# Attention and states @ w1 in small array tiles, x turned on VectorE, every engine in text order, the last states' round in a branch

## The chip, the core and the metric

One core of one Trainium2 chip. The metric is the device time of one execution in microseconds (us); the kernel before took 625.12 (median of 3 runs, 624.7 to 626.98).

## What is computed

```python
# attention block: B=8, H=8, S=512, Ns=32, D=64
scores = 0.125 * x @ state^T            # per (b, h): 512 x 32
xread  = softmax(scores, over states) @ state        # 512 rows per batch
sread  = softmax(scores^T, over tokens) @ x          # 32 rows per batch
rows   = concat([xread, sread], axis=2), heads side by side   # 8 x 544 rows of 512
# routing: E=8 experts, F=1024
logits = rows @ w_gate                  # 512 x 8
e      = argmax(logits);  gw = softmax(logits)[e]
out    = gw * (relu(rows @ w1[e]) @ w2[e])           # w1[e]: 512 x 1024, w2[e]: 1024 x 512
```

All in float32. With the seeded inputs all 512 x rows of a batch go to one expert, and the 256 state rows go to the eight experts as 32, 120, 0, 29, 1, 40, 0, 34. In groups of up to 32 rows of one expert that is 11 groups.

## The kernel before

**Attention** (`front`, `back`, L340 to L366). For each batch, x lies in SBUF with 128 tokens a row (`load_x`, L172, packets of one head's 64 numbers) and is turned on TensorE, 16 transpositions of 128x128 into one PSUM buffer, each four of them copied out on ScalarE (`transpose_x`, L194). The states of a batch are turned on TensorE into `stT`, in which two heads share a 128x64 block with zeros in the other halves (`prep_state`); `scores` multiplies each such block with the turned x into `pc`. `read_weights` makes the softmax over states (32x32 block transpositions and full-width operations on VectorE, exp on ScalarE, one product on GpSimd) and `write_weights` that over tokens. `back` turns the second softmax on TensorE (`transpose_write`), multiplies it with x (`write_rows`, `pw`) and stores the rows to DRAM (`st_dram`, L258), and forms the gate logits of the x rows (`logits_x`, `pl`). `route` and `choose` give each batch its expert `eb`; SyncE reads it into a register (L323) and loads that expert's w1 and w2 (L332, L336).

**Feed-forward of a batch** (`batch`). xread @ w1 is not formed directly: `states_w1` multiplies the states with w1 into `G` (`pG`), `up` multiplies `G` with the softmax (`ph`), and `down` multiplies the result with w2 (`py`). Each 512-column product shows as two MATMULs of 512 columns in the trace.

**State rows.** After all batches' attention, `logits_s` reads the state rows back (`srow`), a rank among the rows of each expert sends them by indirect DMA to slots in `ss_dram`, and four rounds of 128 slots (four groups of 32) run through their own experts' weights: `round_x` turns the rows, `round_up` (`pgh`) and `round_down` (`pgy`) multiply with tiles `s` of four experts (1 MB each, four DMAs on SyncE's queue), four w1 buffers (`S1B`) and three w2 buffers (`S2B`).

**Order.** Only TensorE's instructions keep their text order (`mm`, `tp`, L124, L127); the other engines' are placed by the planner. The attention of batches 0 and 1 runs ahead of the first feed-forward. That of batches 2 to 7 is a generator whose pieces are put between the matmuls of `up` (after each `f`) and `down` (after every second `f`) of batches 0 and 1; what is left of it, `logits_s`, the ranks and the scatter stand after batch 1. The four rounds are a second generator, put between the matmuls of batches 2 to 7. A branch at the end handles x rows whose expert is not their batch's; none are there.

Of the kernel before, what the change touches and what calls it, by code (L numbers as in the profile page):

```python
# [20 lines left out]
def kernel(  # L21
# [15 lines left out]

    nc = tc.nc

# [17 lines left out]
    S1B, S2B = 4, 3  # L57
# [10 lines left out]

    ident = const.tile([128, 128], FP32)
    masks.make_identity(nc, ident[:])  # L70
    iota_p = const.tile([128, 1], FP32)
    nc.gpsimd.iota(iota_p[:], pattern=[[0, 1]], base=0, channel_multiplier=1,
                   allow_small_or_imprecise_dtypes=True)
    colf = const.tile([128, 128], FP32)
    nc.gpsimd.iota(colf[:], pattern=[[1, 128]], base=0, channel_multiplier=0,
# [3 lines left out]
    nc.vector.tensor_scalar(U128[:], colf[:], iota_p[:, 0:1], None, ALU.is_gt)  # L79
    ones_b = const.tile([128, 128], BF16)  # L80
    nc.gpsimd.memset(ones_b[:], 1.0)
    rev8 = const.tile([128, E], FP32)
    nc.gpsimd.iota(rev8[:], pattern=[[-1, E]], base=E, channel_multiplier=0,
                   allow_small_or_imprecise_dtypes=True)
    io8 = const.tile([128, E], FP32)
    nc.gpsimd.iota(io8[:], pattern=[[1, E]], base=0, channel_multiplier=0,
                   allow_small_or_imprecise_dtypes=True)
    jio = const.tile([128, NG], FP32)
    nc.gpsimd.iota(jio[:], pattern=[[1, NG]], base=0, channel_multiplier=0,
# [3 lines left out]
    nc.gpsimd.iota(tok_x[:], pattern=[[SO, B], [1, NC]], base=0, channel_multiplier=NC)  # L93
# [3 lines left out]
    nc.vector.tensor_scalar(quad[:], iota_p[:], 32.0, None, ALU.is_ge)  # L97
    for q in (64.0, 96.0):
        nc.vector.tensor_scalar(tmp_p[:], iota_p[:], q, None, ALU.is_ge)
        nc.vector.tensor_tensor(quad[:], quad[:], tmp_p[:], ALU.add)  # L100
    tok_s = const.tile([128, NST], I32)
    nc.vector.tensor_scalar(tmp_p[:], quad[:], float(SO - NS), iota_p[:, 0:1], ALU.mult, ALU.add)
    for g in range(NST):
        nc.vector.tensor_scalar(tok_s[:, g:g + 1], tmp_p[:], float(4 * g * SO + S), None, ALU.add)

    wg = const.tile([128, NDC, E], FP32)
    nc.scalar.dma_start(out=wg[:], in_=moe_w_gate.rearrange("(c p) e -> p c e", p=128))


    aT = const.tile([128, B, 2, S], FP32)  # L110
    stT = const.tile([128, B, NPR, 2 * NS], FP32)
    NX = B * NC
    lg = const.tile([128, NX + NST, E], FP32)
# [8 lines left out]
    def mm(*args, **kw):  # L122

        tc.keep_in_program_order(nc.tensor.matmul(*args, **kw))  # L124

    def tp(*args):
        tc.keep_in_program_order(nc.tensor.transpose(*args))  # L127

    turn = [0]

    def evict(dst, src):

        turn[0] += 1
        if turn[0] % 2:
            nc.scalar.copy(dst, src)
        else:
            nc.vector.tensor_copy(out=dst, in_=src)  # L137


    ffn = tc.alloc_tile_pool(name="ffn", bufs=1)  # L140
    ps_h = tc.alloc_tile_pool(name="ps_h", bufs=2, space=PSUM)
    ps_y = tc.alloc_tile_pool(name="ps_y", bufs=2, space=PSUM)


    att = tc.alloc_tile_pool(name="att", bufs=2)
    ps_c = tc.alloc_tile_pool(name="ps_c", bufs=1, space=PSUM)
    ps_m = tc.alloc_tile_pool(name="ps_m", bufs=1, space=PSUM)
    ps_s = tc.alloc_tile_pool(name="ps_s", bufs=1, space=PSUM)


    st2 = att.tile([128, B * 2, 2, D], FP32, bufs=1)
    st_rows = state.rearrange("b (g i) n d -> (i n) (b g) d", g=2)
    for u in (slice(0, 2), slice(2, 2 * B)):
        for k in range(2):
            nc.scalar.dma_start(out=st2[:, u, k, :], in_=st_rows[:, u])
    nc.vector.memset(stT[:], 0.0)
    gst = att.tile([128, B, 2, E], FP32, bufs=1)


    blank = att.tile([128, XW], I32, bufs=1)  # L160
    nc.gpsimd.memset(blank[:], 0)
    nc.gpsimd.memset(blank[:, DM + 1:DM + 2], FAR)
    for r in range(NR):
        nc.scalar.dma_start(out=ss_dram[ts(r, 128)], in_=blank[:])

    x_nat = {}

    def load_x(b):

        x_nat[b] = att.tile([128, NC, H, D], FP32, tag="x", bufs=3, name="x_nat")  # L170
        for c in range(NC):
            nc.sync.dma_start(out=x_nat[b][:, c],  # L172
                              in_=x[b].rearrange("h (p c) d -> p c h d", c=NC)[:, c])

    def prep_state(b):
        pt = ps_m.tile([128, 2, 2, 2, NS], FP32, tag="m", name="pt")
        for g in range(2):
            tp(pt[:, g], st2[:, 2 * b + g], ident[:])
        for i in range(2):

            evict(stT[ts(i, 64), b].rearrange("p (g j) n -> p g j n", g=2)[:, :, :, ts(i, NS)],
                  pt[ts(i, 64), :, :, i, :])

        pg = ps_s.tile([128, 2, E], FP32, tag="s", name="pg")
        for j in range(NPR):
            mm(pg[ds(64 * (j % 2), 64), j // 2, :], lhsT=stT[:, b, j, :], rhs=wg[:, j, :],
                             start=True, stop=True, skip_group_check=True)
        evict(gst[:, b], pg[:])

    def transpose_x(b, xT, j):  # L190
        pt = ps_m.tile([128, NC, 128], FP32, tag="m", name="pt")
        for c in range(NC):
            tp(pt[:, c, :], x_nat[b][:, c, ts(j, 2), :], ident[:])
        nc.scalar.copy(xT[:, j], pt[:])  # L194

    def scores(b, xT):

        pc = ps_c.tile([128, 2, S], FP32, tag="c", name="pc")
        for j in range(NPR):
            mm(pc[ts(j % 2, 64), j // 2, :], lhsT=stT[:, b, j, :], rhs=xT[:, j],  # L200
                             start=True, stop=True, skip_group_check=True)
        return pc

    def read_weights(b, pc):

        NB = 2 * S // 32
        sx = att.tile([128, NB, NS], FP32, tag="sx", name="sx")
        nc.vector.transpose(sx[:].rearrange("p b n -> p (b n)"), pc[:].rearrange("p g s -> p (g s)"))
        mx = att.tile([128, NB, 1], FP32, tag="mx", name="mx")
        nc.vector.tensor_reduce(mx[:, :, 0], sx[:], AX.X, ALU.max)  # L210
        nc.vector.tensor_tensor(sx[:], sx[:], mx[:].to_broadcast([128, NB, NS]), ALU.subtract)
        nc.scalar.activation(sx[:], sx[:], AF.Exp, bias=0.0, scale=SCALE)
        sm = att.tile([128, NB, 1], FP32, tag="sm", name="sm")
        nc.vector.tensor_reduce(sm[:, :, 0], sx[:], AX.X, ALU.add)
        nc.vector.tensor_scalar(sm[:], sm[:], 1e-9, None, ALU.add)
        nc.vector.reciprocal(sm[:], sm[:])  # L216
        nc.gpsimd.tensor_tensor(sx[:], sx[:], sm[:].to_broadcast([128, NB, NS]), ALU.mult)  # L217
        nc.vector.transpose(aT[:, b].rearrange("p g s -> p (g s)"), sx[:].rearrange("p b n -> p (b n)"))  # L218

    def write_weights(pc):  # L220

        nm = att.tile([128, 2], FP32, tag="nm", name="nm")
        nc.vector.tensor_reduce(nm[:], pc[:], AX.X, ALU.max)
        nc.vector.tensor_scalar(nm[:], nm[:], -SCALE, None, ALU.mult)
        a2 = att.tile([128, 2, S], FP32, tag="a2", name="a2")
        s2 = att.tile([128, 2], FP32, tag="s2", name="s2")
        for g in range(2):
            nc.scalar.activation(a2[:, g], pc[:, g], AF.Exp, bias=nm[:, g:g + 1], scale=SCALE,
                                 accum_out=s2[:, g:g + 1])
        nc.vector.tensor_scalar(s2[:], s2[:], 1e-9, None, ALU.add)  # L230
        nc.vector.reciprocal(s2[:], s2[:])
        return a2, s2

    def transpose_write(a2):

        a2T = att.tile([128, 2, NC, 128], FP32, tag="a2T", name="a2T")
        for g in range(2):
            pt = ps_m.tile([128, NC, 128], FP32, tag="m", name="pt")
            for c in range(NC):
                tp(pt[:, c, :], a2[:, g, ts(c, 128)], ident[:])  # L240
            nc.scalar.copy(a2T[:, g], pt[:])  # L241
        return a2T

    def write_rows(b, a2T, s2):


        pw = ps_s.tile([128, 2, 2, D], FP32, tag="s", name="pw")
        for g in range(2):
            for c in range(NC):
                for i in range(2):  # L250
                    mm(pw[ts(i, 64), g], lhsT=a2T[:, g, c, ts(i, 64)],
                                     rhs=x_nat[b][:, c, ts(2 * g + i, 2), :],
                                     start=(c == 0), stop=(c == NC - 1), skip_group_check=True)
        xs = att.tile([128, 2, 2, D], FP32, tag="xs", name="xs")
        for g in range(2):
            nc.vector.tensor_scalar(xs[:, g], pw[:, g], s2[:, g:g + 1], None, ALU.mult)
        for i in range(4):
            nc.scalar.dma_start(out=st_dram[ts(b, NS)].rearrange("n (g i d) -> n g i d", g=2, i=4)[:, :, i, :],  # L258
                                in_=xs[ts(i, NS), :, i % 2, :])
# [80 lines left out]
    def front(b):  # L340

        xT = att.tile([128, NPR, NC, 128], FP32, tag="xT", bufs=1, name="xT")
        for j in range(NPR):
            transpose_x(b, xT, j)
            yield
# [420 lines left out]
```

## Time and profile before

| | us |
|---|---|
| profiled execution, device time | 626.47 |
| its span, first to last instruction | 624.6 |
| TensorE MATMUL busy (2225) | 541.8 (87%) |
| VectorE / ScalarE / GpSimd busy | 132.1 / 109.3 / 23.4 |
| `py` / `ph` MATMULs busy | 234.8 (512) / 119.4 (256) |
| `pgh` / `pgy` MATMULs busy | 35.4 (256) / 31.7 (256) |
| `pG` MATMULs busy | 32.4 (128) |
| mean granted TensorE clock | 0.947 |
| HBM read and written | 123 MB, 197 GB/s over the span |

Busy time of a group counts overlapping MATMULs once; the mean duration of one is longer than its share, since the array is pipelined. PEclk is the granted clock: 1.00 is 2.4 GHz, 0.50 is 1.2 GHz, and what lies between is a mean over a stretch. DMA share is the mean busy share of 16 DMA engines.

### The profile page before, as it was taken

Reading aid. Unit: us, or ns where it says so; the run is one execution under the profiler, and the core shown is the slowest. Engines: PE = TensorE matmul, PEld = TensorE weight load, DVE = VectorE, ACT = ScalarE, POOL = GpSimd, SP = SyncE. Lnnn points to the kernel's source line nnn. Section 1 sums busy time; section 2 is a strip of 40 time slices with the busy share of each in tenths; the row PEclk is TensorE's granted clock in tenths of the full one; section 3 lists DMA queues with packets and bytes.
Section 4 is the critical chain, followed back from the end, with each engine's and each line's share of the span. In section 5 each row is a group of like instructions: output and inputs, shape, how many; then the busy total and the mean of one; then the engine's idle time right before and its main releaser. Section 6 shows DMA issues by size and latency. Waiting matters only on the chain.

```text
span 624.6 us, 6270 instructions
## 1 busy us (share of the span) xinstructions
PE 541.8 (87%) x2225; PEld 241.4 (39%) x2225; DVE 132.1 (21%) x287; ACT 109.3 (17%) x202; POOL 23.4 (4%) x29
## 2 busy tenths in 40 slices
PE   1674798988979894858599999999999999999997
PEld 0354344554535552413133343333433333333343
DVE  1245234524634240220001100110011002000100
ACT  1322133324323211110001101110011101101100
POOL 1011001011010010010000000000000000000000
PEclk9967799999999997797989999999999999999999
DMA  9416920464404004049898987999899879534601
GB/s 239 98 41 166 388 89 1 105 206 143 115 6 151 23 20 171 0 168 309 296 356 284 371 318 233 299 356 335 285 323 372 284 271 324 188 115 173 198 25 44
DMA packets 96497, 123.15 MB, mean 197 GB/s; under 512 B 45775, under 2 KB 45775, under 8 KB 96464
## 3 DMA queue, kind: packets, MB, share of 16 engines
q1 hardware_dynamic: 83552, 110.65, 53.6%
q10 hardware_dynamic: 12432, 11.04, 5.3%
q0 software_dynamic: 480, 1.05, 0.5%
q8 instruction: 18, 0.29, 0.2%
q14 instruction: 15, 0.12, 0.1%
HBM read 111.69 MB, written 11.54 MB: 197 GB/s over the span
## 4 chain that ended last, share of the span: by engine, by line
PE 77%; issue 8%; DMA 7%; ACT 4%; DVE 2%; SPq 1%; ACTq 1%; POOL 0%; POOLq 0%; DVEq 0%
PE py L124 34%; PE ph L124 16%; PE pgh L124 6%; PE pgy L124 5%; PE pt L127 5%; PE pG L124 4%; PE pw L124 3%; PE pc L124 2%; DMA w1t<-in_moe_w_dram 2%; PE pl L124 2%; DMA s<-in_moe_w_dram 1%; DMA ss_dram<-blank 1%; DMA ss_dram<-srow,slot_i 1%; ACT xT L194 1%; ACT a2T L241 1%
## 5 line engine op out<-in xcount | busy, mean ns | idle before, releaser
L124 PE MATMUL py<-w2t,hT 128*128 128x512 f32 x512 | 234.8, 604 | 0.0
L124 PEld LDWEIGHTS py<-w2t,hT 128*128 128x128 f32 x512 | 94.0, 192 | 119.7 <-issue 119.7
L124 PE MATMUL ph<-aT,G 128*128 128x512 f32 x256 | 119.4, 610 | 0.0
L124 PEld LDWEIGHTS ph<-aT,G 128*128 128x128 f32 x256 | 47.3, 194 | 59.7 <-issue 58.7
L449 ACT ACTIVATE y<-py,gw 128x512 f32<-128x512 f32 x32 | 22.0, 687 | 223.6 <-PE py L124 211.7
L405 DVE TENSOR_SCALAR hT<-ph 128x512 f32<-128x512 f32 x31 | 21.4, 691 | 153.4 <-PE ph L124 153.4
L124 PE MATMUL pgh<-s,sxT 128*32 128x512 f32 x256 | 35.4, 620 | 6.7 <-DMA s<-in_moe_w_dram 6.7
L127 PE MATMUL pt<-ident,x_nat 128*128 128x128 f32 x128 | 23.2, 306 | 18.3 <-ACT xT L194 9.5
L403 ACT ACTIVATE hT<-ph 128x512 f32<-128x512 f32 x33 | 19.7, 597 | 93.1 <-PE ph L124 93.1
L124 PE MATMUL pG<-w1t,stT 128*64 128x512 f32 x128 | 32.4, 633 | 3.5 <-DMA w1t<-in_moe_w_dram 2.3
L124 PE MATMUL pgy<-s,shT 128*32 128x512 f32 x256 | 31.7, 599 | 0.0
L127 PEld LDWEIGHTS pt<-ident,x_nat 128*128 128x128 f32 x128 | 17.0, 154 | 34.1 <-issue 16.6
L194 ACT COPY xT<-pt 128x512 f32<-128x512 f32 x32 | 18.7, 584 | 32.4 <-PE pt L127 32.4
L217 POOL TENSOR_TENSOR sx<-sx,sm 128x1024 f32<-128x1024 f32 x8 | 15.3, 1912 | 209.1 <-DVE sm L216 186.5
L124 PE MATMUL pl<-gst,aT 128*128 128x8 f32 x128 | 17.1, 270 | 6.0 <-DVE aT L218 6.0
L124 PEld LDWEIGHTS pl<-gst,aT 128*128 128x128 f32 x128 | 16.6, 209 | 11.5 <-issue 11.5
L124 PE MATMUL pw<-x_nat,a2T 128*64 128x128 f32 x256 | 18.9, 311 | 1.7 <-DVE gst L137 1.4
L124 PEld LDWEIGHTS pgh<-s,sxT 128*32 128x32 f32 x256 | 7.9, 111 | 31.9 <-issue 17.6
L127 PE MATMUL pt<-ident,a 128*128 128x128 f32 x64 | 11.5, 306 | 9.6 <-ACT a2T L241 5.4
L124 PEld LDWEIGHTS pw<-x_nat,a2T 128*64 128x64 f32 x256 | 16.9, 159 | 3.3 <-DVE gst L137 1.8
L124 PEld LDWEIGHTS pG<-w1t,stT 128*64 128x64 f32 x128 | 7.8, 141 | 24.7 <-DVE G L137 7.6
L124 PE MATMUL pc<-xT,stT 128*64 128x512 f32 x64 | 17.3, 665 | 0.0
(114 smaller groups left out, 237.8 us busy)
## 6 DMA issues: line engine op xcount, KB each, us to landing
s<-in_moe_w_dram SPq DMA_DIRECT2D x256, 256.0 KB, 5.2
w1t<-in_moe_w_dram SPq DMA_DIRECT2D x8, 2048.0 KB, 9.5
w2t<-in_moe_w_dram SPq DMA_DIRECT2D x8, 2048.0 KB, 10.9
x_nat<-in_x_dram SPq DMA_DIRECT2D x32, 256.0 KB, 4.0
out_dram<-y ACTq DMA_DIRECT2D x32, 256.0 KB, 4.5
ss_dram<-blank ACTq DMA_DIRECT2D x4, 257.0 KB, 6.3
xg<-ss_dram SPq DMA_DIRECT2D x4, 257.0 KB, 3.3
st<-in_state_dram ACTq DMA_DIRECT2D x2, 448.0 KB, 8.7
```

Of the source, the lines that this page charges most:

```text
L124: tc.keep_in_program_order(nc.tensor.matmul(*args, **kw))
L127: tc.keep_in_program_order(nc.tensor.transpose(*args))
L194: nc.scalar.copy(xT[:, j], pt[:])
L217: nc.gpsimd.tensor_tensor(sx[:], sx[:], sm[:].to_broadcast([128, NB, NS]), ALU.mult)
L241: nc.scalar.copy(a2T[:, g], pt[:])
L403: nc.scalar.activation(dst, src, AF.Relu)
L405: nc.vector.tensor_scalar(dst, src, 0.0, None, ALU.max)
L449: nc.scalar.activation(y[:], py[:], AF.Copy, scale=gw[:, NC * b + c, :])
```

## The change

- All engines' instructions go through `InOrder`, which keeps them in text order.
- x is loaded in packets of 1 KB, two DMAs a batch, and turned in 32x32 blocks by VectorE; no TensorE transposition and no ScalarE copy is left for it. The states are loaded four times over (with halves swapped in every second copy) and turned by VectorE.
- Scores: 64 products of 32x32 tiles with 128 columns for each batch in place of 4 of 128x64 with 512. `pw`: 32 products with 32 columns of weights and 64 columns of x in place of 16 of 64 and 128. `pl`: the gate's table is the weight and the softmax the moving side, 8 products of 128 columns, and VectorE turns the result. `pg` and `pG`: 64x32 tiles, `pG` 16 products of 512 columns a batch in place of 8.
- PSUM: four banks for `pG`, `ph`, `py` together, four for the attention (`pa`).
- relu runs on ScalarE alone. In attention behind the first three fronts a subtraction moves from VectorE to GpSimd.
- Batches 0 and 1 choose their expert ahead of their state rows. Attention 2 to 7, `logits_s`, ranks, scatter and the rounds are one generator (`others`); its pieces stand after every fourth matmul of `down` and every second `f` of `up` of all eight batches: 12 a batch.
- Three rounds run always; the fourth stands in a branch that is taken when there are more than 12 groups. `S1B` goes from 4 to 3.

```diff
+        def __getattr__(self, name):
+            def call(*args, **kw):
+                ins = getattr(self.engine, name)(*args, **kw)
+                tc.keep_in_program_order(ins)
+                return ins
+            return call
...
+    NRS = 3
+    S1B, S2B = 3, 3
...
+    def load_x(b):
+        x_nat[b] = att.tile([128, H, NC, D], FP32, tag="x", bufs=2, name="x_nat")
+        for h in (slice(0, 4), slice(4, 8)):
+            sp.dma_start(out=x_nat[b][:, h].rearrange("p h c d -> p h (c d)"),
+                         in_=x[b, h].rearrange("h (p c) d -> p h (c d)", c=NC))
...
+    load_x(0)
+    load_states(0, 1)
+    load_x(1)
...
+    def front(b, early):
+
+        xt = att.tile([128, H, NC, 2, 32], FP32, tag="xt", name="xt")
...
+            if h.start == 4:
+                dve.transpose(stT[:, b].rearrange("p h u n -> p (h u n)"),
+                              st4[:, ts(b, H)].rearrange("p h d -> p (h d)"))
+            dve.transpose(xt[:, h].rearrange("p h c u t -> p (h c u t)"), x_nat[b][:, h].rearrange(flat))
+            yield
+
+        for q in range(4):
+            for g in range(2):
+                pe.matmul(pa[ts(q, 32), 2 + g, 1, 0:E], lhsT=stT[ts(g, 64), b, 2 * q + g, 0, :],
+                          rhs=wg[ts(g, 64), q, :], start=True, stop=True, skip_group_check=True)
         for g in range(2):
...
+            for u in range(2):
+                for q in range(4):
+                    for i in range(4):
+                        pe.matmul(pa[ts(q, 32), i, 0, ts(g, 128)],
+                                  lhsT=stT[ts(i, 32), b, 2 * q + g, u ^ (i % 2), :],
+                                  rhs=xt[ts(i, 32), 2 * q + g, :, u, :],
+                                  start=(u == 0), stop=(u == 1), skip_group_check=True)
...
+                for q in range(4):
+                    pe.matmul(pw[ts(q, 32), g], lhsT=a2T[:, g, c, ts(q, 32)], rhs=x_nat[b][:, 2 * q + g, c, :],
+                              start=(c == 0), stop=(c == NC - 1), skip_group_check=True)
...
+        for q in range(4):
+            sp.dma_start(out=st_dram[ts(b, NS), ts(q, 128)], in_=xs[ts(q, 32)].rearrange("p g d -> p (g d)"))
+        if b + 2 < B:
+            load_x(b + 2)
...
+        for g in range(2):
+            for i in range(4):
+                pe.matmul(pl[ts(i, 32)], lhsT=gst[:, b, g, :], rhs=aT[:, b, i, g, :],
+                          start=(g == 0), stop=(g == 1), skip_group_check=True)
+        dve.transpose(lg[:, ts(b, NC)].rearrange("p c e -> p (c e)"), pl)
...
+        for k in range(2):
+            pg = [ps_p.tile([128, 512], FP32, tag="p", name="pG") for _ in range(2)]
+            for q in range(4):
+                for g in range(2):
+                    pe.matmul(pg[g][ts(q, 32), :], lhsT=st[ts(g, 64), 2 * q + g, 0, :],
+                              rhs=w1t[ts(g, 64), q, ts(k, 512)], start=True, stop=True, skip_group_check=True)
...
+            if insert and f % 2:
                 insert()
...
+                if insert and f == 3:
                     insert()
...
+            for k in range(NDC):
+                round_up(r, k)
+                fetch(2, 0)
+                yield
+                if k % 2:
+                    yield
+            round_h(r)
+            yield
+            for f in range(0, NFC, 2):
+                for i in range(2):
+                    round_down(r, f + i)
+                    fetch(0, 1)
+                yield
+                if f % 4:
+                    yield
...
+    for _ in front(0, True):
+        pass
+    for _ in run(front(1, True), back(0, True)):
+        pass
     e0 = expert_of(eb, 0)
     load_w1(0, e0)
     load_w2(0, e0)
+    for _ in run(front(2, True), back(1, True)):
+        pass
     load_w2(1, expert_of(eb, 1))
...
+        for b in range(2, B):
+            yield from run(*([front(b + 1, False)] if b + 1 < B else []), back(b, False))
+        yield from logits_s()
+        yield from sort_states()
+        change_pools()
+        yield from rounds(0, NRS)
...
+        with tc.If(number(more_i, NG) > 0):
+            for _ in rounds(NRS, NR):
+                pass
```

In text order, `front` of the first two batches and `back` go on as: full-width VectorE steps of the first softmax, the second softmax's exps on ScalarE, then for `back(0)` the turned softmax, logits, `route`, `choose`, and after the scores of the next batch the state rows, their four stores and the next `load_x`, all three on SyncE's queue ahead of the first w1.

## Rows read from the trace of the kernel before

**Rows 1.** Busy time by stretch: engines' busy us (instructions), granted clock, DMA share, GB/s.
```profile
0.00:67.50 67.50, 33.06 (x188) 22.54 (x188) 25.32 (x72) 14.32 (x29) 5.92 (x17) 0.80 0.60 154
67.50:236.00 168.50, 154.04 (x789) 80.91 (x790) 68.21 (x134) 50.32 (x101) 11.47 (x6) 0.99 0.32 104
236.00:320.00 84.00, 56.91 (x175) 24.50 (x174) 9.94 (x40) 7.10 (x12) 2.13 (x2) 0.80 0.62 209
350.00:500.00 150.00, 148.54 (x557) 55.21 (x559) 15.33 (x22) 18.59 (x30) 1.96 (x2) 1.00 0.91 316
```
**Rows 2.** The same for single tiles: py twice, ph twice, pG, pgh.
```profile
67.50:236.00 168.50, 59.93 (x128) 22.39 (x128) 4.81 (x7) 0.99 0.32 104
236.00:320.00 84.00, 20.89 (x42) 8.55 (x42) 2.06 (x3) 0.80 0.62 209
67.50:236.00 168.50, 30.44 (x65) 11.19 (x66) 5.52 (x8) 4.78 (x8) 0.99 0.32 104
236.00:320.00 84.00, 16.51 (x32) 6.76 (x31) 2.08 (x3) 2.98 (x5) 0.80 0.62 209
67.50:236.00 168.50, 13.21 (x48) 3.20 (x48) 4.15 (x6) 3.40 (x6) 0.99 0.32 104
236.00:320.00 84.00, 10.43 (x48) 2.40 (x48) 0.00 (x0) 0.00 (x0) 0.80 0.62 209
```
**Rows 3.** The chain of waits inside the first feed-forward batches: start us, us, what.
```profile
74.81 0.44 PE pt L127 x4
75.25 1.72 PE ph L124 x4
...
84.40 0.41 PE pg L124 x8
84.81 1.91 PE ph L124 x4
86.72 1.87 PE pc L124 x8
...
107.29 1.97 PE pw L124 x32
...
113.04 1.88 PE pl L124 x16
```
**Rows 4.** Tile pgh in slices of 10 ns, where one group of four tiles begins.
```profile
378.27:378.28 0.01, 0.00 (x1) 0.00 (x1) 0.00 (x0) 0.00 (x0) 1.00 0.00 0
...
378.29:378.30 0.01, 0.01 (x4) 0.01 (x4) 0.00 (x0) 0.00 (x0) 1.00 0.00 0
```
**Rows 5.** Timeline of the start: start us, us, engine (q: its DMA queue), line, operation.
```profile
1.28 3.83 ACTq L155 DMA_DIRECT2D st<-in_state_dram  x4
...
5.62 8.28 ACTq L164 DMA_DIRECT2D ss_dram<-blank  x4
...
29.65 1.24 DVE L208 STREAM_TRANSPOSE sx<-pc 128x1024 f32<-128x1024 f32 x1
...
54.63 0.14 DVE L320 CAST eb<-eb_f 128x1 int32<-128x1 f32 x1
...
57.70 0.39 SPq L332 DMA_DIRECT2D w1t<-in_moe_w_dram  x1
...
67.54 5.36 PE L124 MATMUL pG<-w1t,stT 128*64 128x512 f32 x16 [2.34 <-DMA w1t<-in_moe_w_dram]
```
**Rows 6.** The chain of waits again, from the scatter into the rounds.
```profile
272.79 7.53 DMA ss_dram<-srow,slot_i
...
304.87 6.71 DMA s<-in_moe_w_dram
...
323.42 1.85 PE pgh L124 x16
```
**Rows 7.** DMA issues of the rounds' weight tiles: count, KB each, us to landing.
```profile
s<-in_moe_w_dram SPq DMA_DIRECT2D x256, 256.0 KB, 5.2
```

More of the change, by code (lines that the diff above doesn't have):

```diff
@@ L134, in evict @@
         if turn[0] % 2:
-            nc.scalar.copy(dst, src)
+            act.copy(dst, src)
         else:
[L137 to L162, printed above, removed]
@@ L190, in transpose_x @@
[L190 to L202, printed above, removed]
@@ L286, in route @@
+        yield
+        for t in range(NST):
+            for c in range(NDC):
+                pe.matmul(pl[:, t, :], lhsT=sT[:, t, c, :], rhs=wg[:, c, :],
+                          start=(c == 0), stop=(c == NDC - 1), skip_group_check=True)
+        dve.tensor_copy(out=lgs[:], in_=pl)
+        route(lgs[:], NX, NST)
+        yield
+    def route(lg, u0, U):
         r = slice(u0, u0 + U)
         mx = att.tile([128, U, 1], FP32, tag="r_mx", bufs=1, name="r_mx")
-        nc.vector.tensor_reduce(mx[:, :, 0], lg[:, r], AX.X, ALU.max)
+        dve.tensor_reduce(mx[:, :, 0], lg, AX.X, ALU.max)
@@ L386, in run @@
             yield
-    def attention(b0, b1):
-        yield from front(b0)
-        for b in range(b0, b1):
-            yield from run(*([front(b + 1)] if b + 1 < b1 else []), back(b))
-            finish(b)
     def no_dep(d):
@@ new lines, with change_pools, round_in @@
+    late = {}
+    def change_pools():
+        ps_a.release()
+        att.release()
+        late["sst"] = tc.alloc_tile_pool(name="sst", bufs=1)
+        late["ps_g"] = tc.alloc_tile_pool(name="ps_g", bufs=1, space=PSUM)
+        late["ps_t"] = tc.alloc_tile_pool(name="ps_t", bufs=1, space=PSUM)
+    rd = [dict() for _ in range(NR)]
+    def round_in(r):
+        xg = late["sst"].tile([128, XW], FP32, tag="xg", bufs=2, name="xg")
+        sp.dma_start(out=xg[:].bitcast(I32), in_=ss_dram[ts(r, 128)])
+        rd[r].update(xg=xg, e=[expert_of(eg, 4 * r + q) for q in range(4)])
@@ new lines, in round_w1, with round_w2 @@
+    def round_w1(r, k, half):
+        t = late["sst"].tile([128, 4, 512], FP32, tag="s1", bufs=S1B, name="s1")
+        for q in range(4):
+            sp.dma_start(out=t[:, q], in_=moe_w1[ds(rd[r]["e"][q], 1), ts(k, 128), ts(half, 512)]
+                              .rearrange("o p f -> p (o f)"))
+        rd[r][1, k, half] = t
+    def round_w2(r, f):
+        t = late["sst"].tile([128, 4, DM], FP32, tag="s2", bufs=S2B, name="s2")
+        for q in range(4):
+            sp.dma_start(out=t[:, q], in_=moe_w2[ds(rd[r]["e"][q], 1), ts(f, 128), :]
+                              .rearrange("o p f -> p (o f)"))
+        rd[r][2, f] = t
@@ new lines, in round_x, with round_up @@
+    def round_x(r):
+        pt = late["ps_t"].tile([128, NDC, 128], FP32, tag="t", name="ptx")
+        for c in range(NDC):
+            pe.transpose(pt[:, c, :], rd[r]["xg"][:, ts(c, 128)], ident[:])
+        xT = late["sst"].tile([128, NDC, 128], FP32, tag="sxT", bufs=2, name="sxT")
+        evict(xT[:], pt[:])
+        rd[r]["xT"] = xT
+        rd[r]["ph"] = [late["ps_g"].tile([128, 512], FP32, tag="g", bufs=2, name="pgh") for _ in range(2)]
+    def round_up(r, k):
+        for half in range(2):
+            for q in range(4):
+                pe.matmul(rd[r]["ph"][half][ts(q, 32), :], lhsT=rd[r]["xT"][:, k, ts(q, 32)],
+                                 rhs=rd[r][1, k, half][:, q, :], start=(k == 0), stop=(k == NDC - 1),
+                                 skip_group_check=True)
@@ L482, in batch @@
             hT = up(G, aT[:, b + 1], piece)
+    work = others()
     G = states_w1(w1s[0], stT[:, 0])
@@ L486 @@
     hT = up(G, aT[:, 0], piece)
-    batch(0)
-    batch(1)
+    for b in range(B):
+        batch(b)
     for _ in work:
@@ L493 @@
     left = const.tile([128, 1], FP32)
[L494 removed]
+    dve.tensor_reduce(left[:], cmx[:, :, 0], AX.X, ALU.add)
     left_i = const.tile([128, 1], I32)
[L496 to L505 removed]
@@ L735 @@
+    for pool in (late["ps_t"], late["ps_g"], late["sst"], ps_p, ffn):
         pool.release()
```

712 lines of the change are left out of this document (321 added, 391 removed).

## The prediction

> **What bounds the kernel now.** I read the page first (TensorE busy 87%, the others near 20%), then the span by stretch, because a mean over stages with different limits says nothing [rows 1]. Four stretches: to 67.5 us TensorE is busy half the time at a mean clock of 0.80, ahead of the first product with w1; to 236 us it works at full clock on batches 0 and 1 with the attention of 2 to 7 between; to 320 us it is busy 56.9 of 84 us at 0.80; from there it is full (148.5 of 150 us) at 316 GB/s, and so to the end. So TensorE's own work is the bound outside two stretches, and there it waits for chains. Next the single tiles in these stretches [rows 2], the chain of waits inside the feed-forward [rows 3], the start's timeline [rows 5] and the chain around the scatter [rows 6].
>
> The unit: four MATMULs of 512 columns take 1.72 us [rows 3], 0.43 each.
>
> **The change part by part.** The sum is made against the profiled execution: 626.5 us, span 624.6.
>
> *Start.* Before, ScalarE issues DMAs until 5.62 + 8.28 = 13.9 us, and eb, w1's issue and the first product stand at 54.6, 57.7 and 67.5 [rows 5]. After, ScalarE has 17 issues instead of 9; four cost 3.83 [rows 5], so I put its first work at 18 us (14 to 22). Then in text order, each full-width step at the 1.24 of the block transposition [rows 5]: the exp, the sum and the product of the softmax with small steps, 5 us; x(1)'s first half and the turned softmax, 2.5; logits, route and choose with some 15 small steps of 0.2, 4.5: eb stands near 30. But SyncE reads it only behind batch 0's stores, and these wait for the scores of batch 1 and four more full-width steps (32 to 40), so w1 is issued near 46 instead of 57.7. Its landing, 10 us [rows 5], isn't last any more: ahead of the first product TensorE has the scores of batch 2 in its order, whose x is issued behind the stores at about 43 and lands some 5 us later; x, the turned softmax, batch 1's logits and choice, and the second half of x follow on VectorE one after another, to 56, and the scores with `pw` end near 59. First product at 59 (55 to 67): **-8.5 us**.
>
> *Attention among the feed-forward.* From 67.5 to 236 TensorE does 128 + 65 products of 0.43 = 83.0 and 13.2 of `pG` [rows 2]. The rest of the 168.5, 72.3 us or 12 a batch, is attention and what it makes TensorE wait. A batch has 16 transpositions of x (four cost 0.44), the states' turn with its wait for two copies, `pc` 1.87, `pw` 1.97, `pl` 1.88 and the transpositions of the second softmax [rows 3]. After: no transposition of x or states. Scores are 64 products, so 128 MATMULs of 128 columns, 0.43 / 4 = 0.11 each alone. No row shows tiles with fewer than 128 rows. The nearest is `pgh`, four column tiles at once: 16 MATMULs in 1.85 [rows 6], begun within 30 ns of each other [rows 4]. With four at a time the scores take 128 x 0.11 / 4 = 3.5 us, with 16 at a time 0.9; I take 1.2, since starts at most 10 ns apart leave 128 of them 1.3 at most. `pw`: 64 MATMULs of 64 columns, four at a time, 0.9 to 1.0. `pl`: 16 of 128 columns, four at a time, 0.45 (its 1.88 is loads of 128 columns of weights for 8 columns of work). `pg` 0.3 (0.41 now), the eight transpositions 0.9, the count 0.1. Each return from small tiles to full ones costs 1.91 - 1.72 = 0.2 [rows 3], five or six a batch: 1.2. That makes 5.2 a batch; six batches less one front are 30: **-42** (-46 to -27).
>
> The Trainium skill says the opposite of a free mix: a change of tiling mode, not of the tile alone, drains TensorE (TensorEngine Tiling (Array Packing), Key Properties). Here a drain is no more than the 0.2 of the first `ph` behind `pg`; by the rule with that row the new 64x32 and 32x32 blocks add six such drains a batch, the 1.2 above, and nothing else.
>
> VectorE takes 3 us a batch more for x and states (1.24 for 1,024 columns), on a stretch where it is busy 68 of 168 us; ScalarE loses four copies and gets the other half of the relus. Six pieces a batch of 3.4 us of matmuls cover both. If that cover goes, `scores` waits, the third rival.
>
> *States @ w1.* `pG` is 16 MATMULs a batch; of three in 13.2 us the first took 5.4 at a low clock [rows 2, 5], so 3.9 when warm. After: 32 of 512 columns in 64x32 tiles, eight at a time, 32 x 0.43 / 8 = 1.7 and a switch, 1.9. If row halves take turns it is 3.4. Eight batches save 16, less 1 for a first one that is still cold: **-15** (-16 to -2).
>
> *Between batch 1 and the rounds.* From 236 to 320 TensorE does 42 + 32 products of 0.43 = 31.8, `pG` 3.9, 48 MATMULs of `pgh` 5.6 [rows 2, 6], in all 41.6 with the first turn of rows. So 42.4 us are lost: the state rows' way through DRAM, the scatter (7.53) and first weight tiles (6.71) [rows 6], and half clock behind the gaps. After, that chain lies between matmuls of batches 2 and 3. 96 pieces stand in the text (4 in the first `up`, 8 in each `down`, 4 in each further `up`); the generator needs 87, of which 35 attention, 6 logits and ranks, 3 spare pieces ahead of the rounds. So nothing is left over at the end. 3.5 us of logits and turns remain. What is late next are weight tiles. The first four of w1 need a buffer that the first product frees, behind three tiles of w2: as now, 7. Then with three buffers the second half of the next step's w1 is fetched only when the step's first half is done. It has one piece (3.44) and two halves of 0.93, 5.3 us, where 1.3 us of issue and 5.2 of landing are needed [rows 7]; steps with two pieces have 8.7. 12 of 24 steps are short by about 1.3: 15 us (0 to 45). Remaining 25.5: **-17** (-35 to +10). The DMA rate itself suffices: 50 MB of three rounds, 11 of batches' weights and 6 of rows in about 215 us are 312 GB/s, where 316 ran without a stop [rows 1].
>
> *Fourth round.* 11 groups fit into three rounds. A round is eight blocks of 16 MATMULs at 1.85 [rows 6], 12 transpositions at 0.11, two waits for a copy and eight returns of 0.2, 19 us, all between dense matmuls: **-19** (-16 to -20). Relu of a round on ScalarE alone, one after the other at TensorE's cost: **+2**.
>
> *Text order.* Nothing is queued past what waits, so a late step holds its whole engine. Where pieces are 3.4 us apart most steps are done a piece early; I take **+5** (0 to 30) for the rest.
>
> Sum: -8.5 - 42 - 15 - 17 - 19 + 2 + 5 = -94.5. 626.5 - 94.5 = 532.0; the median of the runs is 1.4 below the profiled one: **530 us**.
>
> **The rivals.**
> 1. *Weight tiles bound the rounds.* All 24 steps wait, the short ones for 3 us, the long ones for 1, instead of 15 in all 48: +33, 563. For it: the buffers went from four to three and pieces came closer. Against it: in 350 to 500 TensorE kept 99% at 316 GB/s [rows 1].
> 2. *Row groups take turns*, only column tiles run at once: scores 3.5 instead of 1.2, `pG` 3.4 instead of 1.9, eight batches: +30, 560. For it: no row shows two row groups. Against: the tiles' results go to different PSUM banks.
> 3. *Text order holds the engines.* The start gains nothing (+8.5) and each of six attention batches stops four pieces by 0.7 us, about half a full-width step of VectorE (+17): +25, 555.
> 4. *One tile at a time*, at the scores and `pG`: 128 x 0.11 and 32 x 0.43 are 13.8 us each, `pw` 3.5, `pl` 1.7, in all 33 a batch instead of 4.6. Eight batches: +227, 757, slower than before. It decides from below two tiles at a time on: 33 / 1.9 is 17.3 a batch, 102 us over the forecast, and all is gone. Against: four column tiles do run at once [rows 4], so row tiles would have to break that.
> 5. *A fixed cost per instruction.* If each MATMUL cost 62 ns, 128 scores would be 7.9 us: +54, 584. [rows 4] show four begun in 30 ns, and eight of `pg` with their weights took 0.41 [rows 3], which leaves it one chance in a hundred. The Trainium skill gives these 62 ns as what the sequencer spends on a MATMUL where hardware decode is off (TensorE: Matmul & The Clock Gate, "Wait — 56ns, not 53.3ns?"); by that rule the forecast would be 584, and the trace speaks against its condition.
> 6. *The branch is taken* (the change wouldn't do what it says): a round's 16.8 MB alone at 316 GB/s is 53 us with nothing beside it: 583. The routing counts above exclude it unless float rounding moves a row; one in a hundred.
>
> **How the numbers follow.** Chances: forecast 0.64, weights 0.12, row groups 0.10, text order 0.10, one tile 0.02, fixed cost 0.01, branch 0.01. The range goes down to 500, where start, attention and weights all come out at their good ends (-4, -4, -17, and text order free, -5), and up to 566, beyond the first three rivals. Faster by over 0.5% (about what a measurement here can tell from no change) is all but the one-tile case and a remainder: 0.97; same 0.01; slower 0.02.
>
> **What would show it.** Start: the first `pG` near 59. Attention: the scores' 128 MATMULs of a batch in about 1.2 us; 3.5 says rival 2, 14 rival 4. `pG` 1.9 a batch. Middle: no stretch with TensorE below 90% between the first product and the end but for waits on `s`, in sum near 22 us, and no half clock there. Rounds: 192 MATMULs of `pgh`, not 256. Wrong would be: the first product at 67 or later; waits on `s` above 40 us; TensorE waiting for VectorE's turned x in the feed-forward; any `pgh` behind the last `py`.

## The result, and the profile after

The changed kernel takes 608.24 us (median of 4 runs, 605.07 to 611.25), beside 626.05 for the kernel before on the same chip: 0.971 of it (0.966 to 0.977), 18 us faster. The forecast was 530, with a range of 500 to 566. The sign was right; 78 of the 96 us forecast did not come. The profiled execution took 607.1 us, its span is 605.3.

The span by stretch, with the columns of [rows 1]; the stretches are the start, the attention of batches 2 to 7, the sort, the first round's products with w1, the rest of the rounds, the end.

```profile
0.00:79.60 79.60, 20.66 (x616) 15.32 (x616) 40.87 (x91) 10.66 (x21) 2.09 (x15) 0.98 0.63 160
79.60:306.00 226.40, 193.67 (x1748) 91.66 (x1752) 78.30 (x176) 54.38 (x104) 19.11 (x10) 0.92 0.31 107
306.00:325.00 19.00, 19.00 (x77) 8.09 (x62) 5.50 (x30) 2.76 (x5) 2.13 (x2) 1.00 0.62 214
325.00:383.00 58.00, 46.97 (x173) 15.86 (x171) 2.08 (x3) 9.48 (x16) 0.00 (x0) 0.91 0.88 303
383.00:562.70 179.70, 171.72 (x666) 61.63 (x665) 6.34 (x9) 25.15 (x41) 1.96 (x2) 0.99 0.78 264
562.70:605.30 42.60, 37.98 (x90) 16.58 (x88) 1.15 (x4) 6.33 (x10) 0.98 (x1) 1.00 0.08 29
```

TensorE stands still in three places: the start is 12 us longer than before, the attention stretch has gaps and a clock of 0.92, the first round waits. The same for `py` and `ph` alone, as in [rows 2]:

```profile
79.60:306.00 226.40, 89.26 (x192) 36.65 (x192) 8.24 (x12) 0.92 0.31 107
79.60:306.00 226.40, 64.54 (x128) 25.87 (x128) 19.11 (x32) 0.92 0.31 107
```

320 products of 0.43 are 137.6 us, and four and a half `pG` of 1.9 some 8.5; 80 of the 226.4 us are attention and its waits, where the terms had 30 and 3.5. One of five equal places, TensorE's timeline (in brackets the idle time ahead and who ended it):

```profile
96.83 0.27 PE L48 MATMUL pa<-wg,stT 64*32 64x8 f32 x16
97.03 1.90 PE L48 MATMUL pa<-xt,stT 32*32 32x128 f32 x128
103.15 0.75 PE L48 MATMUL pa<-aT,gst 128*32 128x128 f32 x16 [4.21 <-DVE nm L48]
103.83 5.24 PE L48 MATMUL ph<-aT,G 128*128 128x512 f32 x8
111.09 0.24 PE L48 MATMUL pa<-oh,ones_b 128*128 128x8 bf16 x4 [2.02 <-ACT a L48]
```

The logits (`pa<-aT,gst`) need nothing of `nm`, the maxima over the scores just computed. But these belong to the next batch, lie in the first halves of the same four banks of `pa`, and the logits are written into a second half. VectorE shows what TensorE sat through:

```profile
99.17 1.44 DVE L48 STREAM_TRANSPOSE sx<-pa 128x256 f32<-128x256 f32 x4 [5.30 <-ACT gst L48]
100.65 1.22 DVE L48 TENSOR_REDUCE mx<-sx 128x32 f32<-128x1024 f32 x1
101.78 1.22 DVE L48 TENSOR_REDUCE nm<-pa 128x2 f32<-128x1024 f32 x1
```

The next eight `ph` then took 5.24 us instead of the 3.7 that they take at full clock behind small tiles, at a granted clock of 0.70. What TensorE waited for, over the whole span (us, times, longest), and in the last line the copies `a2T` in the attention stretch alone:

```profile
PE pa L48 <- DVE nm L48: 21.1, 5, 4.2
PE pa L48 <- ACT sx L48: 10.9, 2, 5.4
PE pa L48 <- ACT a2T L48: 7.0, 10, 0.7
PE pa L48 <- ACT a L48: 6.7, 3, 2.6
...
PE pa L48 <- ACT a2T L48: 4.2, 6, 0.7
```

The waits for `nm` and `a` all stand in the attention stretch, the two for `sx` at the start.

At the start [rows 5], ScalarE's queue, its first copy `gst`, then the table's `eb`, w1's issue and the first product:

```profile
0.76 5.39 ACTq L48 DMA_DIRECT2D st<-in_state_dram  x6
7.11 0.40 ACTq L48 DMA_DIRECT2D wg<-in_moe_w_gate_dram  x1
7.55 13.52 ACTq L48 DMA_DIRECT2D st<-in_state_dram  x6
21.16 2.62 ACTq L48 DMA_DIRECT2D ss_dram<-blank  x4
...
25.16 0.17 ACT L48 COPY gst<-pa 128x16 f32<-128x16 f32 x1
...
40.58 0.15 DVE L48 CAST eb<-eb_f 128x1 int32<-128x1 f32 x1
41.45 0.39 SPq L48 DMA_DIRECT2D w1t<-in_moe_w_dram  x1
...
76.43 1.22 DVE L48 TENSOR_REDUCE nm<-pa 128x2 f32<-128x1024 f32 x1
76.55 1.06 ACT L48 ACTIVATE sx<-sx 128x1024 f32<-128x1024 f32 x1 [4.02 <-DVE sx L48]
77.75 1.93 PE L48 MATMUL pa<-x_nat,a2T 128*32 128x64 f32 x64 [5.44 <-ACT sx L48]
79.62 3.62 PE L48 MATMUL pG<-w1t,stT 64*32 64x512 f32 x32
```

The view puts the wait of `pw` down to ScalarE's exp `sx`, which neither reads `pa` nor makes anything that `pw` needs. `nm` reads `pa` and ended 0.04 us later (77.65 and 77.61).

In the rounds, the idle time ahead of instructions on tile `s`, and a piece of the chain of waits [rows 6]:

```profile
  DMA s<-in_moe_w_dram: 41.8, 35
```
```profile
331.60 6.35 DMA out_dram<-y
...
340.95 6.48 DMA s<-in_moe_w_dram
347.48 1.91 PE pgh L48 x2
349.39 3.64 PE py L48 x8
```

### The profile page after: what moved, and what is told of

Same layout as the page of the kernel before. It is cut to its first block, busy times and chain, and to the rows that moved or that the text cites. A ratio compares the mean times of both kernels' runs of the same rounds, so it can differ in the third digit from the quotient of the medians.

```text
span 605.3 us, 8328 instructions
## 1 busy us (share of the span) xinstructions
PE 490.0 (81%) x3353; PEld 209.1 (35%) x3353; DVE 134.2 (22%) x312; ACT 108.8 (18%) x197; POOL 26.3 (4%) x30
## 4 chain that ended last, share of the span: by engine, by line
PE 69%; DMA 12%; DVE 8%; ACT 4%; ACTq 3%; SPq 2%; issue 2%; POOL 0%; POOLq 0%; DVEq 0%
PE py L48 33%; PE ph L48 17%; PE pa L48 8%; DMA s<-in_moe_w_dram 7%; PE pgy L48 4%; PE pG L48 3%; PE pgh L48 3%; ACTq L48 3%; DVE sx L48 3%; DMA out_dram<-y 2%; SPq L48 2%; DVE mx L48 2%; DVE nm L48 1%; DMA st<-in_state_dram 1%; ACT a2T L48 1%
## 5 line engine op out<-in xcount | busy, mean ns | idle before, releaser
L48 ACT ACTIVATE hT<-ph 128x512 f32<-128x512 f32 x64 | 38.2, 597 | 115.2 <-PE ph L48 115.2
L48 PE MATMUL pa<-aT,gst 128*32 128x128 f32 x128 | 7.4, 369 | 49.0 <-DVE aT L48 28.0
L48 DVE COPY G<-pG 128x512 f32<-128x512 f32 x16 | 10.8, 687 | 65.1 <-PE pG L48 65.0
L48 DVE STREAM_TRANSPOSE sx<-pa 128x256 f32<-128x256 f32 x32 | 11.5, 417 | 45.3 <-ACT gst L48 45.3
L48 DVE STREAM_TRANSPOSE xt<-x_nat 128x1024 f32<-128x1024 f32 x16 | 19.5, 1218 | 5.2 <-DMA x_nat<-in_x_dram 5.2
L48 PE MATMUL pa<-x_nat,a2T 128*32 128x64 f32 x512 | 10.5, 244 | 10.9 <-ACT sx L48 10.9
L48 PE MATMUL pG<-w1t,stT 64*32 64x512 f32 x256 | 18.9, 706 | 0.0
L48 PE MATMUL pa<-xt,stT 32*32 32x128 f32 x1024 | 18.5, 329 | 0.2 <-DVE xt L48 0.2
L48 POOL TENSOR_TENSOR sx<-sx,mx 128x1024 f32<-128x1024 f32 x5 | 9.6, 1911 | 179.0 <-DVE mx L48 179.0
L48 PE MATMUL pa<-ident,a 128*128 128x128 f32 x64 | 12.0, 318 | 6.2 <-ACT a2T L48 5.6
L48 DVE TENSOR_SCALAR xs<-pa,s 128x64 f32<-128x64 f32 x16 | 3.8, 280 | 55.1 <-ACT hT L48 20.3
```

Of the source, the lines that this page charges most:

```text
L48: ins = getattr(self.engine, name)(*args, **kw)
```

## The experiments

Times of a kernel stand beside those of the kernel before on its own chip; the ratio is to it, in brackets its interval (after: 0.971).

### The order of logits and scores

```
-    for _ in run(front(1, True), back(0, True)):
+    for _ in run(back(0, True), front(1, True)):
```
and so for the other two calls.

> Edit: in each turn of the interleaving, the piece of the batch in the back half (logits, count, pw) stands ahead of the piece of the batch in the front half (scores). Theory A, shared PSUM banks: logits, count and pw are written into the second halves of the same four banks that hold the scores, and TensorE must not write a bank while VectorE or ScalarE still read it. In the trace of the changed kernel pl waits 4.5 us five times for the second maximum over the scores (nm), pr 2.6 to 3.2 us three times for ScalarE's exp over them, pw 5.4 us twice ahead of the first product. With the order swapped these find the banks read out: 22 + 8.5 + 11 = 41 us less waiting, part of which comes back where the scores then wait for the copy or the turn of pl: 30 to 45 us faster, 563 to 578 us, and the half clock behind the gaps (103 to 254 us in the trace) is gone. Rival B, late data: pl waits because turn_read and the softmax are late on VectorE, whatever the banks; then the waits are as long in the new order or longer: 600 to 615 us. Rival C, text order on VectorE and ScalarE holds the engines: the waits only change places, 595 to 612 us.

577.9 us, 0.923 (0.919 to 0.928): 30 us less. The same place of its timeline:

```profile
96.53 0.64 PE L48 MATMUL pa<-aT,gst 128*32 128x128 f32 x16
97.61 0.28 PE L48 MATMUL pa<-wg,stT 64*32 64x8 f32 x16 [0.44 <-DVE lg L48]
97.82 1.90 PE L48 MATMUL pa<-xt,stT 32*32 32x128 f32 x128
99.65 3.70 PE L48 MATMUL ph<-aT,G 128*128 128x512 f32 x8
103.85 0.26 PE L48 MATMUL pa<-oh,ones_b 128*128 128x8 bf16 x4 [0.50 <-DVE nm L48]
```

The wait of 4.2 us is gone, and `ph` is back at full clock. What is left are 0.4 us that `pg`, which goes to banks 2 and 3 of `pa`, waits for the turn of the logits into `lg`, which reads bank 1. The gain could still be the order and not the shared tile, which the next run tells apart.

### Other PSUM tiles, the same order

```
-        pl = pa[:, 1, 1, 0:128]
+        pl = ps_p.tile([128, 512], FP32, tag="p", name="pl")[:, 0:128]
```
and so for `pr` and `pw`.

> Edit: the results of the logits (pl), the count (pr) and pw lie in the buffers of the feed-forward's PSUM pool, in other banks than the scores; the order of the text stays. Theory A, shared banks: the waits of pl (4.5 us five times), pr (2.6 to 3.2 us three times) and pw (5.4 us twice) go as in the run with the swapped order, though nothing on VectorE or ScalarE comes earlier; the four buffers are shared by one more user, which costs up to 5 us: 575 to 588 us. Rival B, the swapped order gained because VectorE and ScalarE had other work first, not because of the banks: 600 to 612 us.

570.7 us, 0.908 (0.906 to 0.911): 37 us less, better than expected.

```profile
91.95 0.27 PE L48 MATMUL pa<-wg,stT 64*32 64x8 f32 x16
92.15 1.90 PE L48 MATMUL pa<-xt,stT 32*32 32x128 f32 x128
93.98 0.64 PE L48 MATMUL pl<-aT,gst 128*32 128x128 f32 x16
94.56 3.70 PE L48 MATMUL ph<-aT,G 128*128 128x512 f32 x8
100.40 0.26 PE L48 MATMUL pr<-oh,ones_b 128*128 128x8 bf16 x4 [2.15 <-DVE oh L48]
```

The logits follow the scores at once, with the same work ahead of them on every engine. So the wait came from sharing `pa`. What is left, 2.15 us for `oh`, is data.

This run moves the results into another tile and other banks at once. The changed kernel's own rows tell that the waits go by the tile:

```profile
123.54 0.60 PE L48 MATMUL pa<-ident,a 128*128 128x128 f32 x4
124.18 0.58 ACT L48 COPY a2T<-pa 128x512 f32<-128x512 f32 x1 [3.18 <-PE pa L48]
124.82 0.66 PE L48 MATMUL pa<-ident,a 128*128 128x128 f32 x4 [0.68 <-ACT a2T L48]
```

The first four transpositions go to banks 0 and 1, and the copy reads these; the next four go to banks 2 and 3, need nothing of the copy, and wait for it all the same. In no trace with this tile does a write of TensorE into `pa` overlap a read of it by another engine, whatever the banks. `nm` and `a` read all four banks, so keeping engines apart by bank alone would have made the same logits and counts wait. A tile for each bank was not tried.

### The states' loads on another queue

```
-    load_states(1, B)
+    load_states(1, B, sp)
-        act.dma_start(out=ss_dram[ts(r, 128)], in_=blank[:])
+        sp.dma_start(out=ss_dram[ts(r, 128)], in_=blank[:])
```

> Edit: the loads of the states of batches 1 to 7 and the four stores of blanks are issued by SyncE instead of ScalarE. Theory A: ScalarE's 17 DMA issues, each waiting for one of eight DMA semaphores that SyncE's transfers use too, hold its queue until 23.9 us, where I had put 18; gst, and behind it the turn of the scores, come only at 25.2 though the scores are done at 17.2. Without them gst is at 18 to 19 and the first product about 6 us earlier (76 to 70 instead of 79.6 us from the span's start): 600 to 604 us. Rival B: the start is set by the chain of bank waits and by x(2), loaded at 56 behind batch 0's stores; then the first product moves by less than 2 us, or comes later as x and the stores of batch 0 stand behind the states on SyncE: 606 to 612 us.

599.4 us, 0.960 (0.955 to 0.965): 9 us less. `gst` stands at 17.3 instead of 25.2, the first `pG` at 72.0 instead of 79.6. The shared semaphores of theory A are not what held the queue for most of that time: in the changed kernel the last four of the six later issues found their semaphore's transfer landed 2 us or more before. One issue by itself took up to 3.6 us, where those of a single batch's states took 0.3 to 0.5.

### The weight tiles of the rounds: a fourth buffer, and longer steps

The first edit is `S1B, S2B = 4, 3`; the second, alone:

```
                 yield
-                if k % 2:
-                    yield
+                yield
```

> Edit: four buffers for the tiles of w1 in the rounds instead of three (room made by two buffers of y instead of three and one of the turned rows instead of two). Theory A, buffers: in the rounds TensorE stands 42 us for tiles of w1 and w2 (35 waits), where my forecast had 22; the second half of w1 is fetched only when the first half of the step before frees a buffer. With a fourth buffer these waits fall to 20 to 25: 588 to 598 us. Rival B: the tiles wait behind the stores of y, which take 6 to 7 us each between 331 and 360 and share the eight DMA semaphores with them: the waits stay near 40, 604 to 612 us; a single y buffer less may add some.

> Edit, to the changed kernel: in the rounds every step with tiles of w1 is followed by two pieces of the batches' work, where every other step had one (six pieces more in the rounds, six fewer behind them, where 39 us of such work stand with nothing to wait for). Theory A, the forecast's mechanism: short steps have 5.3 us of work for 6.5 us of issue and landing; with 8.7 us everywhere the waits for s fall from 42 us to 20 to 28, and the kernel takes 592 to 600 us. Rival B, the rate or the order of the transfers is the limit (stores of y between, eight shared semaphores): the waits move to the next steps and the sum stays, 604 to 610 us.

593.7 us, 0.951 (0.947 to 0.955), and 592.1 us, 0.943 (0.936 to 0.951). The waits on `s`, with the fourth buffer and with longer steps:

```profile
  DMA s<-in_moe_w_dram: 19.7, 28
```
```profile
  DMA s<-in_moe_w_dram: 24.9, 21
```

From 41.8 either way, by two edits that leave the stores of `y` where they are (the first even takes one of their buffers). So the stores in the chain are not what holds the tiles; the short steps are, as the forecast had it, only at a higher price.

### All engines but TensorE free of the text

> Edit: only TensorE is kept in the order of the text; VectorE, ScalarE, GpSimd and SyncE are ordered by the planner again. Theory A, shared PSUM banks: the scores' readers are needed by pl, pr and pw whatever order VectorE and ScalarE take, so the planner gains at most what it moves ahead of other work: 600 to 615 us. Rival C, text order holds the engines: pl waits 4.5 us because VectorE's nm stands behind the turn, the maximum and the subtraction of the same batch, and loads wait behind stores on SyncE; free of the text the waits shrink: 570 to 590 us.

582.7 us, 0.933 (0.928 to 0.938): rival C's range, though what theory A names stays. `PE pa <- DVE nm` is 18.4 us in five waits, and the waits on `s` are 41.2. What went are `pr`'s waits for ScalarE's exponentials `a`, which the text puts behind relus, and half of `pw`'s at the start (2.9 us instead of 5.4, twice): `nm` now runs ahead of the other maximum and the subtraction. `pw` starts there at 51.4 and the exp `sx` at 53.7, so it was not `sx` that `pw` waited for.

### Three rounds in the kernel before

> Edit, to the kernel before: only three of the four rounds stand in the program (the fourth has no rows with these inputs). The forecast's term for the fourth round was 19 us of TensorE's work between dense matmuls. Theory A: the term is right, 604 to 609 us. Rival B: the fourth round lay beside waits, or its pieces of matmul work were what covered the weight tiles, so that less than half goes: 614 to 622 us. Rival C: with its 16.8 MB of weights the DMA rate eases too and the first three rounds gain: 596 to 603 us.

606.8 us, 0.967 (0.965 to 0.969): 20.3 less than the kernel before, where the term had 19.

### Together

> Edit: the swapped order, the states' loads and the blanks on SyncE, and four buffers for w1's tiles together. Theory A, the three losses lie in three stretches (attention, start, rounds) and add: 30.3 + 8.8 + 14.5 us from 608.2 gives 554.6, 550 to 559 us. Rival B: they share covers (the s tiles' waits move with the pieces of attention, SyncE's queue holds x and the states): two thirds of the sum, 565 to 575 us.

557.6 us, 0.889 (0.886 to 0.893). The three losses nearly add: 30.3, 8.8 and 14.5 alone, 53.6 in sum, 50.6 together.

> Edit: as the run with the three edits together, and VectorE, ScalarE, GpSimd and SyncE ordered by the planner (TensorE by the text). Theory A, what the planner gave alone (25.5 us) was mostly another order of the readers of the same banks and an earlier start, which the three edits have already: 545 to 556 us. Rival C, text order on the other engines costs something of its own beside the banks, 10 us or more of it in the feed-forward and the rounds: 530 to 544 us.

547.9 us, 0.875 (0.872 to 0.878): 10 us less, the price of the text's order beside the three edits, and in theory A's range. It lies behind the start, where the first `pG` comes later (72.5 instead of 66.5). From there to the first turn of rows it takes 211.6 us instead of 219.1, and from that to the last `pgy` 217.9 instead of 226.1; the relu `sh`, which TensorE awaited 4.8 us in three rounds, is late no longer.

### What a MATMUL in a 32x32 tile costs

```
-  rhs=xt[ts(i, 32), 2 * q + g, :, u, :],
+  rhs=xt[ts(i, 32), 2 * q + g, 0, u, :],
```

> Edit, to the changed kernel: each MATMUL of the scores multiplies 32 columns (tokens) instead of 128; the other three quarters of the scores stay zero, so routing differs and only the scores' own time is read (16 pg and 128 score MATMULs, 2.05 us with 128 columns at full clock). Theory A, the columns set the time, with fewer tiles at a time than 16: about a quarter for the scores, 0.5 to 0.8 us in all. Theory B, one tile's weight load (104 ns) and MATMUL follow one another, 8 of each a tile: the 107 ns of 128 columns become 27, so 1.2 to 1.5 us. Theory C, a cost of each MATMUL or load, about 14 ns, whatever the columns: 1.9 to 2.1 us.

One run, read at the scores alone:

```profile
130.39 0.27 PE L48 MATMUL pa<-wg,stT 64*32 64x8 f32 x16
130.59 1.29 PE L48 MATMUL pa<-xt,stT 32*32 32x32 f32 x128
```

1.29 us instead of 1.90, in theory B's range. Each of 16 tiles has eight of the 128 MATMULs, so 96 columns cost 0.61 / 8 = 76 ns, 0.8 ns a column, which is the rate of a full product (0.43 us for 512). All 16 tiles do run together. The rest, 1.90 / 8 - 0.101 = 0.136 us for each MATMUL in its tile, does not depend on columns. One load of weights for such a tile takes 0.104; that it is this load is near, not shown. The Trainium skill gives a MATMUL some 60 cycles of overhead (TensorEngine Tiling (Array Packing), Instruction Overhead), by estimate 25 ns at 2.4 GHz; here it is 0.136 us, several times that, though a weight load may be part of it.

### The first product earlier, and the best kernel

Logits, count and `pw` in other PSUM tiles, the states, the fourth buffer and the planner in one kernel:

> Edit: logits, count and pw in the feed-forward's PSUM buffers (order of the text unswapped), states' loads and blanks on SyncE, four buffers for w1's tiles, and all engines but TensorE ordered by the planner. Theory A, the banks are the whole of what the swapped order gained, and the rest adds as before: the buffers gained 7 us more than the order alone, so 540 to 548 us against 547.9. Rival B: with the swapped order and the planner the waits were gone already and the shared buffers only cost: 549 to 556 us.

553.4 us (0.877 to 0.887): rival B's range. The 5 us behind the swapped order are not clear of noise (0.872 to 0.878 there); `pr` now waits 14.0 us for `oh`. Then the first product ahead of batch 1's logits, in that kernel and in the one with the swapped order:

> Edit: as the run before, and the first product with batch 0's expert stands in TensorE's text ahead of batch 1's logits and batch 2's scores, which become pieces of its own feed-forward. Theory A: nothing of the data holds the first product; w1 of batch 0 is issued at 43 us at the latest and its 2 MB land 10 us later, so pG starts at 50 to 55 us instead of 72 and the wait of 14 us for batch 1's turned softmax lies beside matmuls: 522 to 532 us. Rival B: pieces of the first up wait for batch 1's softmax (TensorE's order is the text's), w1 of batch 1 comes late behind w2 of batch 0 on the queue, and half of it comes back: 534 to 542 us.

> Edit: as the run of the three edits with the planner (547.9 us), and the first product ahead of batch 1's logits and batch 2's scores. Theory A, the run with the early product lost its gain to logits and counts that stand behind the scores (pr waits 4 us four times): with the swapped order 528 to 540 us. Rival B, the five pieces that moved from the start into the feed-forward are missing behind the rounds or delay them, and the gain is given back as waits for s: 544 to 552 us.

552.7 us (0.878 to 0.887) and 544.8 (0.869 to 0.874). `pG` began at 44.1 and 53.0 instead of 66.4 and 72.5, yet next to nothing came of it: the first run is slower than both of its ranges, the second is in rival B's. Five pieces more stand ahead of the rounds, and the waits on `s` rose from 22.8 to 37.7 us and from 23.4 to 35.4.

> Edit: as the run of the three edits with the planner (547.9 us), and two pieces behind every step with tiles of w1. Theory A, the 23 us of waits for s that are left there come from short steps: 8 to 14 us less, 534 to 540 us. Rival B, four buffers had covered those already; what is left is the first tiles and the half clock behind them: 544 to 550 us.

542.9 us, 0.867 (0.865 to 0.869), between the two ranges and the fastest here: 65 us below the changed kernel, 13 above the forecast. Waits on `s` are 17.4 us. Its span by stretch:

```profile
0.00:72.50 72.50, 20.09 (x605) 15.08 (x605) 38.70 (x92) 9.32 (x19) 2.10 (x15) 0.65 0.72 184
72.50:285.00 212.50, 201.35 (x1823) 95.38 (x1824) 79.36 (x207) 58.53 (x111) 21.26 (x12) 0.98 0.39 131
285.00:500.00 215.00, 210.87 (x810) 78.83 (x809) 8.42 (x12) 37.46 (x61) 1.96 (x2) 1.00 0.80 278
500.00:541.50 41.50, 36.85 (x119) 14.31 (x117) 0.75 (x1) 3.94 (x6) 0.98 (x1) 0.98 0.45 154
```

## Why the prediction was wrong

*Attention, -42: the step that failed.* It counted TensorE's MATMULs and put every wait at nothing, with "Six pieces a batch of 3.4 us of matmuls cover both". Pieces cover a wait for data, which comes a piece later; they cover no wait between two results of one piece. The prediction even counted banks in the tiles' favour ("the tiles' results go to different PSUM banks"), and never asked what else lies in them.

Before, the scores had a PSUM tile of their own, and logits, count and `pw` took turns in another; after, all share `pa`, so logits of one batch wait for the readers of the next batch's scores. The runs with another order and with other tiles both take the waits for `nm` away, and no other edit does; those for `a` also go when the planner orders the other engines. Between the first `pG` and the first turn of rows the other order gives back 27 us and the other tiles 31 (218.7 and 214.8 instead of 245.5).

Of the 46.5 us missing, TensorE stood idle for 32.7 (226.4 less 193.7): 21.1 for `nm`, 6.7 for `a`, 4.9 for the copies `a2T` and, for the state rows, `sT`. No term had any of these, and the last are no price of the change: the kernel before waits 6.1 us for `a2T`. Some 13 more are what MATMULs behind the waits took above their times at full clock: 1.6 to 3.0 behind each wait for `nm`, and 1.6 of one `pG` behind a wait for `a`. The MATMULs themselves cost what the terms had: scores with `pg` 0.5 a batch more, the returns to full tiles less, 0.1 each. That is 46 of the 46.5.

The Trainium skill has a rule that bears on this (PSUM — Partial Sum Buffer, PSUM bank collisions raise a hardware error): engines are to be kept apart by bank and 32 partitions, not by address. By it logits and `nm` had to be kept apart, which was not weighed. The traces agree in so far as the logits write other bytes than `nm` reads and waited 4.2 us, and did not wait for it in another tile; that the waits also stand between banks of one tile (0.68 us above) is more than the rule asks for.

*Start, -8.5; measured +12.1.* The mark for a wrong forecast, a first product at 67 or later, was hit. ScalarE was put free at 18 us (14 to 22) from four issues in 3.83 us; it was free at 23.9, since the second six issues took 13.5 us. Moved away, they gave 7.6 us, and with all three edits `eb` stood at 31.6, where the step had "near 30". The shared tile cost 5.4 twice, where `pw` waits for `nm` of the next batch; the swapped order gave 5.9 of that (first product at 73.7). Of the remaining 7.5 us (66.5 against 59) a part are small tiles that run slower there than later: batch 2's scores take 2.8 us instead of 1.90 and `pw` 1.93 instead of 1.10.

*Between batch 1 and the rounds, -17.* Waits on `s` were put at 22 us, 15 of it for the short steps, with 45 as their far end: measured 41.8. The mechanism was right, both runs on it say so; the price was towards the far end. The mark "above 40" for a wrong forecast was hit. The rival that weight tiles bound the rounds named the buffers too, at +33; the waits here were 20 above the forecast's, and a buffer or a piece more took 22 or 17 of them away.

*Text order, +5 (0 to 30).* 10 us beside the other edits, 25 alone: in the range, too low. The rival had part of the mechanism: alone, the planner's order brought the first product 3.7 us forward (75.9) and took the waits for `a` away. It had looked for the rest in VectorE's steps.

*Right:* the fourth round, -19 (20.3); `pG`, 1.9 us (rows of 1.95 with the mode's return); no `pgh` behind the last `py`, 192 of them; row groups do run together, 62 ns per MATMUL are not seen (128 in 1.90 us is 15), the branch stayed untaken. No rival alone would have given 608; those below it (555 to 584) all kept the attention term.

*The sum.* Start 20.6, attention 46.5, rounds and what stands with them some 8: the 75 us by which the profiled execution (607.1) missed 532.0. In these 8 the waits on `s` are 20 too many; 12 came out below the terms elsewhere, which no run takes apart. With order, queue, buffers, planner and longer steps changed, the best kernel comes to 542.9.

## What to carry to other kernels

When results that did not share a PSUM tile are moved into one, list who reads the tile and when, and what is written next into it; here a write waited for every reader of the tile, also of other bytes and other banks. A cover of matmuls hides a wait only if it stands between the two instructions in the engine's order, so walk that order past every wait once. And an earlier start can be worth next to nothing where the pieces that it moves stand ahead of waits for transfers: here 12 to 15 us of it came back as waits on `s`; where the rest went was not traced.

## What the runs showed of the hardware

- A wait of 4.2 us on TensorE was followed by a stretch at a granted clock of 0.70, a mean of its two levels (1.2 and 2.4 GHz): eight full products took 5.24 us instead of 3.7. With the slow MATMULs behind it, each of the five gaps cost 1.4 to 1.7 times its length.
- The granted clock does not tell of every slow stretch. The scores of batch 2 with their `pg` at the start, and of a later batch (us from the start, columns as above), stand at 1.00 both, and take 3.1 and 2.1 us; what differs in the rows is what TensorE did ahead of them, waits at the start and full products later.

```profile
69.20:72.35 3.15, 3.07 (x144) 2.36 (x144) 0.00 (x0) 0.00 (x0) 0.00 (x0) 1.00 0.90 316
96.80:98.95 2.15, 2.13 (x145) 1.76 (x144) 0.00 (x0) 0.60 (x1) 0.00 (x0) 1.00 0.77 237
```

- Issuing a DMA can hold its engine for long: the six loads of the states of seven batches (packets of 128 and 256 bytes) took 13.5 us to issue on ScalarE's queue, and 13.0 on SyncE's, up to 3.6 us for one of them. The cost went with the loads; only the engine behind them changed.
- 16 tiles of 32x32 keep the full rate per column, but each MATMUL in its tile costs 0.136 us besides, perhaps its weight load: for 128 fp32 columns more than the columns' own 0.10.
